# Second tile: the turning of batch 2's q waits for the remainder of its v, and the first tile's output is stored behind it

## The chip, the core and the metric

The kernel runs on one core of a Trainium2 chip. A core has a matrix engine (TensorE, PE in the profile, with PEld for its weight loads), a vector engine (DVE), a scalar engine (ACT), GpSimd (POOL) and a queue engine (SyncE, SP). Here POOL and SP mostly start transfers: POOL starts the loads, SP starts the stores and the transfers that transpose ("turn") 16-bit data on the way. The metric is the device time of one execution in microseconds.

## The reference

```python
# q, k, v: [8 batches, 8 heads, 576 rows, 64]; g_norm: [64]
kv  = einsum('bhsd,bhse->bhde', k, v)              # 64 x 64 for each batch and head
o   = einsum('bhsd,bhde->bhse', q, kv)
o   = o / sqrt(mean(o * o, axis=-1) + 1e-6) * g_norm
x   = o.transpose(0, 2, 1, 3).reshape(4608, 512)   # heads side by side
h   = x @ w_in                                     # 512 -> 2048
out = (h * sigmoid(1.702 * h)) @ w_out             # 2048 -> 512, float32
```

## The kernel before, in words

**Tiles.** A batch has 576 rows. Tiles t = 0 to 7 take 512 rows of batch t, tile 8 takes the 64 rows that are left of each of the eight batches. For every tile the kernel multiplies x by w_in (`Hidden` for tile 0, `SevenIn` from tile 1), applies the gate on ACT, and multiplies by w_out (`project_all` for tile 0, `Seven` from tile 1). From tile 1 on both products are done with seven half-size products in place of eight, which takes sums of quarters of the weights (`ws`, `tw`), of x (`xS`) and of the gated values (`gS`), made by DVE.

**Attention runs ahead.** While tile t is multiplied, pieces of the attention of batch t+1 and t+2 are put between the matmuls. The order is written out by hand: `manual_schedule`, and the dictionaries `u1` and `u2`. `at1(i, f)` calls f behind step i of the product with w_in, `at2(i, f)` behind matmul i of the product with w_out. Each engine runs its own instructions strictly in the order in which these calls emit them.

**What a batch from batch 2 on needs.** k and v are loaded by POOL into the two buffers `kraw` and `vbuf`, which all batches share. `load_kv` issues the main part (512 rows: line 115) and the remainder (64 rows: line 120); for batch 2 the main part comes in two halves. `kv_product` (line 247) multiplies k by v: 40 small matmuls, eight with the main rows and then two with the remainder for each pair of heads. q is loaded by `load_q` (line 143 for the main part, 149 for the remainder `qrem`) into `qraw` for even batches and `qbuf` for odd ones. SP turns the main part of q by `transpose_q` (line 290, into `qTd`) and the remainder by `transpose_rest` (line 294, into `qTr`). `rows` (line 332) multiplies the turned q by kv, `out` for the remainder is line 306. `turn` (line 362 on DVE, 368 on SP) scales the rows and turns them into `xT`, which is the next tile's x.

**The second tile, t = 1.** Steps 0 to 27 of its product with w_in are written in `SECOND`. Behind step 5 come `transpose_q` and `transpose_rest` of batch 2; at the step named `kv` stands the product of batch 2's k and v; behind step 22 POOL loads k, v and q of batch 3. In the product with w_out, `rows` of batch 2 stand behind matmul 19, its remainder behind 46, its `turn` behind 40 to 52; behind matmul 88 stands the k-v product of batch 3, behind 89 the loads of batch 4, behind 100 the turning of batch 3's q. In the third tile the k-v product of batch 4 stands behind matmul 15 of the product with w_out.

**Queues.** SP runs its transfers in this order around the change: the eight stores of tile 0 (`store_early(0)`, line 843, called at the end of `layers(0)`; 1 MB of float32 in all), the turning of batch 2's q and its remainder, the two `turn` transfers of batch 2's x, the turning of batch 3's q and remainder, the eight stores of tile 1. Loads from POOL are the software queue (q0) of the profile, transfers from SP and ACT the hardware queue (q1). Both run on the same 16 DMA engines. POOL has one marker form already, in later tiles: `after_turn` and `after_queries` (lines 127 and 131) copy one element of a turned buffer, so that the loads behind them are not issued until it has landed.

Of the kernel before, what the change touches and what calls it, by code (L numbers as in the profile page):

```python
# [16 lines left out]
def kernel(  # L17
# [10 lines left out]
    nc = tc.nc  # L28

    B, H, S, D = q.shape  # L30
# [11 lines left out]
    EARLY = 2  # L42
# [65 lines left out]
    kv_rows = {n: raw[n].rearrange("p c x -> p (c x)") for n in "kv"}  # L108
    RW = J * D
    RS = H * RW  # L110
# [26 lines left out]
    def q_rows(b):  # L137

        rows = qbuf if b % 2 else qraw.rearrange("p c x -> p (c x)")
        return rows[:, 0 : H * J * D]  # L140
# [14 lines left out]
    for n in "kqv":  # L155
# [11 lines left out]
        out=ident,  # L167
        in_=ident,
# [52 lines left out]
    class Attention:  # L221
# [63 lines left out]
                    r = slice(hl * D, (hl + 1) * D)  # L285
                    copy(self.engine, self.kb[to, c0:c1, half, 1 - hl], self.kvp[r, c0:c1, :])

        def transpose_q(self):
            self.qTd = attn.tile([P, H * J // 2, P], F16, name="qTd", tag="qTd", bufs=1)
            nc.sync.dma_start_transpose(out=self.qTd, in_=q_rows(self.b))  # L290

        def transpose_rest(self):
# [447 lines left out]
    def hid_seven(t, hid, seven, units1):  # L740


        xs = made.pop(t, None) or Sums(t, hid.x)
        todo = plan(t)
        parts = [SevenIn(hid, xs, g, todo) for g in range(len(PARTS))]

        def product(step):
            return parts[int(step[0])].product(int(step[1]))

        gates = []  # L750
        for n, step in enumerate(todo.steps):
            behind, gates = gates, []
            if step != "kv":
                gate = product(step)
                if gate:
                    gates.append(gate)
            for u in behind:
                u()
            for u in units1.get(n, ()):
                u()  # L760
            for i in range(4):
                if todo.xsums[i] == n:
                    xs.form(i)
            for i0, i1, which in todo.ready.get(n, ()):
                seven.sums(i0, i1, which)
        for u in gates:
            u()

        def late(step):
            gate = product(step)  # L770
            if gate:
                gate()

        left = {n: [lambda x=x: late(x) for x in steps] for n, steps in todo.late.items()}
        end = lambda: seven.sums(HF - 2, HF, 0)
        if left:
            left[max(left)].append(end)
        else:
            end()
        return left  # L780

    def layers(t, units1, units2):
        hid = d0 if t == 0 else Hidden(t)
        seven = Seven(t, hid.gT) if t else None
        left = hid_seven(t, hid, seven, units1) if t else first_columns(hid, units1)
        osbs[t] = opool.tile([P, 4, DM], F32, name="osb", tag="osb")
        if t:
            todo = {n: [lambda x=x: seven.sums(*x) for x in xs] for n, xs in plan(t).later.items()}
            for n, us in units2.items():
                todo.setdefault(n, []).extend(us)  # L790
            for n, us in left.items():
                todo[n] = us + todo.get(n, [])
            seven.run(todo)
        else:
            project_all(hid.gT, units2)
        if t < EARLY:
            store_early(t)
        elif t < B and t not in HALVED:
            store(t, 0, J)

    def first_columns(hid, units):

        for i, fo in enumerate(COLS):
            if i >= GROUP:
                for ko in range(KO):
                    hid.mm(ko, fo)
                hid.gate(fo)
            for u in units.get(i, ()):
                u()
# [166 lines left out]
    HALVED = (2, 3, 4, 5)  # L976
# [5 lines left out]
    for t in range(NT):  # L982
        b = t + 1
        u1, u2 = {}, {}

        def at1(i, f, *args):
            u1.setdefault(i, []).append(lambda: f(*args))

        def at2(i, f, *args):
            u2.setdefault(i, []).append(lambda: f(*args))  # L990

        def of(b, name, *args):
            return lambda: getattr(live[b], name)(*args)

        if t == 0:
            for l in range(2):
                at1(6, nc.vector.memset, kvd[l], 0.0)
            at1(7, of(0, "out", NPAIR))
            at1(7, scale_w_in, 0, 4)
            at1(7, w_in_sums, 0, 2)  # L1000
            at1(8, start, 1)
            at1(12, scale_w_in, 4, 6)
            at1(12, w_in_sums, 2, 3)
            at1(13, load_q, 2)
            at2(4, setattr, a0, "ss_pool", Attention.ss_pool)
            at2(4, of(0, "ss", NPAIR, True))
            at2(4, of(0, "apply", NPAIR))
            at2(18, weight_sum, 0, 0, HF)
            at2(18, scale_w_in, 6, 8)
            at2(18, w_in_sums, 3, 4)  # L1010
            for c in range(NPAIR):
                at1(12, of(1, "pack_q", c))
                at2(9 + 3 * c, of(1, "q", c))
                at2((36, 36, 49, 49)[c], of(1, "kv", c))
                at2((41, 43, 54, 55)[c], of(1, "out", c))
                at2((45, 50, 58, 60)[c], of(1, "ss", c))
                at2((48, 52, 58, 62)[c], of(1, "apply", c))
            for n in range(1, 4):
                at2(19, weight_sum, n, 0, 4)
                at2(38, weight_sum, n, 4, 6)  # L1020
            at2(39, load_kv, 2, 0, H // 2, False)
            at2(51, clear_rest)
            at2(51, load_kv, 2, H // 2, H)

            def first_sum():
                made[1] = Sums(1, xT[1])
                made[1].form(0)

            at2(55, first_sum)
        elif b < B:  # L1030
            todo = plan(t)
            at = todo.attn
            if t == 1:
                at1(todo.steps.index("kv"), of(b, "kv_all", "D"))
                at1(5, start, b)
                at1(5, of(b, "transpose_q"))
                at1(5, of(b, "transpose_rest"))
                at1(4, nc.scalar.preload_act_table_set, "gelu_apprx_sigmoid_and_others")
                for n, i in ((1, 8), (2, 11), (3, 16)):
                    at1(i, weight_sum, n, 6, HF)  # L1040
                at1(22, load_kv, 3)
                at1(22, load_q, 3)
                at2(88, start, 3)
                at2(88, of(3, "kv_all", "A"))
                at2(89, load_kv, 4)
                at2(89, load_q, 4)
            elif t + 2 < B:
                at2(at["rows"][0], start, t + 2)
                at2(at["rows"][0], of(t + 2, "kv_products"))
                at2(52, of(t + 2, "kv_copies", "A"))  # L1050
                if t + 3 < B:
                    at2(at["rows"][0], load_kv, t + 3, 0, H, False, "k")
                    at2(101, after_turn, b)
                    at2(101, load_kv, t + 3, 0, H, True, "v")
                    at2(101, after_queries, t + 2)
                    at2(101, load_q, t + 3)
            if t + 2 < B:
                at2(49 if t > 1 else 100, of(t + 2, "transpose_q"))
                at2(100, of(t + 2, "transpose_rest"))
            at2(at["table"], nc.scalar.preload_act_table_set, "abs_reciprocal_sqrt_and_small")  # L1060
            for h in range(2):
                at2(at["roots"][h], of(b, "roots", h))
            for j in range(J):
                if j < J // 2:
                    at2(at["rows"][j], of(b, "rows", j))
                for name in ("add_up", "turn"):
                    at2(at[name][j], of(b, name, j))
            rest = (80, 90, 96, 97) if 1 < t < B - 2 else (46, 74, 80, 82)
            at2(rest[0], of(b, "out", NPAIR))
            at2(rest[1], of(b, "ss", NPAIR))  # L1070
            at2(rest[2], of(b, "apply", NPAIR))
            at2(rest[3], nc.scalar.preload_act_table_set, "gelu_apprx_sigmoid_and_others")
        elif t < B:
            for name in ("ss_pool", "rest_pool"):
                at2(16, setattr, live[1], name, (ps_a, "att"))
            at2(16, of(1, "out", NPAIR))
            at2(34, nc.scalar.preload_act_table_set, "abs_reciprocal_sqrt_and_small")
            at2(44, of(1, "ss", NPAIR))
            at2(50, of(1, "apply", NPAIR))
            at2(52, nc.scalar.preload_act_table_set, "gelu_apprx_sigmoid_and_others")  # L1080
        layers(t, u1, u2)


# [28 lines left out]
```

## Time and profile before

| | |
|---|---|
| time, median of 3 runs | 259.11 us (258.80 to 259.48) |
| the profiled execution's own time | 259.74 us |
| span of that execution, first to last instruction | 258.0 us |
| outside the span in that execution | 1.74 us |
| busy share of the span: DVE, ACT, POOL | 75%, 69%, 22% |
| mean granted TensorE clock | 0.993 of full speed |
| DMA | 35.33 MB, mean 137 GB/s |

The views used below: the page (busy time by engine, and the chain of waits that ended last), the chain of waits in order of time (start in us from the beginning of the span, length in us, what), the timeline of one engine in a window (start, length, engine, line, operation), the list of DMA issues in a window (line, queue, count, KB of one, median us from issue to landing), and the stretches (in each of them the busy time of every engine, with the number of instructions, then the granted clock, the mean busy share of the DMA engines and GB/s; that share can exceed 1 because packets overlap on an engine). A length of an SP or POOL row of a transfer is the time that its issue took, not that of the transfer.

### The profile page before, as it was taken

The numbers are of one execution on the slowest core, as the hardware profiler recorded it, in microseconds if no ns is written. First come the engines' busy times: TensorE is split into PE (matmuls) and PEld (weight loads), VectorE is DVE, ScalarE is ACT, GpSimd is POOL, SyncE is SP. The second block draws the span as 40 slices with busy tenths as digits, with TensorE's granted clock in tenths as the row PEclk, the third lists the DMA queues.
The fourth block names the chain that finished last, engine by engine and source line by source line (L and its number), as shares of the span: only waits on it lengthen the run. The fifth ranks groups of instructions, "written<-read, shape, count | busy, mean of one in ns | idle before, by whom it ended". The sixth has DMA issues, their size and how long they took to land.

```text
span 258.0 us, 6355 instructions
## 1 busy us (share of the span) xinstructions
PE 251.7 (98%) x2596; PEld 204.4 (79%) x2596; DVE 193.9 (75%) x344; ACT 177.1 (69%) x322; POOL 57.0 (22%) x92
## 2 busy tenths in 40 slices
PE   8899999999999999999999999999999999999994
PEld 2444454788888888888888888898888888888883
DVE  1546685899958986798679867987799787857872
ACT  3458743988758894899579957995799469536800
POOL 8773244208061013301150134000000000000013
PEclk9979999999999999999999999999999999999999
DMA  7999999999989979996999699909500430012005
GB/s 181 194 188 206 204 204 197 216 216 115 184 159 208 221 91 224 153 158 81 186 184 164 84 205 135 190 5 136 202 4 0 84 163 3 0 57 108 3 19 145
DMA packets 68687, 35.33 MB, mean 137 GB/s; under 512 B 37970, under 2 KB 66258, under 8 KB 68402
## 3 DMA queue, kind: packets, MB, share of 16 engines
q0 software_dynamic: 37632, 18.31, 55.3%
q1 hardware_dynamic: 30624, 16.29, 27.4%
q8 instruction: 20, 0.33, 0.5%
q10 hardware_dynamic: 402, 0.33, 0.5%
q14 instruction: 9, 0.07, 0.1%
HBM read 36.70 MB, written 9.44 MB: 179 GB/s over the span
## 4 chain that ended last, share of the span: by engine, by line
PE 93%; DMA 4%; issue 0%; POOL 0%; DVE 0%
PE o L704 38%; PE h L584 38%; PE hT L473 6%; PE o L819 5%; DMA vbuf<-in_v_dram 2%; DMA qraw<-in_q_dram 2%; PE kvp L247 2%; PE outR L332 1%; PE ss L379 1%; PE outT L302 1%; PE q L454 0%; PE kvp L259 0%; PE outT L306 0%; PE kv L259 0%; DVE osb L684 0%
## 5 line engine op out<-in xcount | busy, mean ns | idle before, releaser
L561 ACT ACTIVATE gT<-h 128x512 f16<-128x512 f32 x96 | 52.5, 601 | 5.6 <-PE h L584 5.6
L584 PEld LDWEIGHTS <-ws 128*128 128x128 f16 x512 | 50.1, 98 | 5.9
L704 PEld LDWEIGHTS <-gS 128*128 128x128 f16 x512 | 49.1, 98 | 6.1 <-DVE gS L636 0.3
L584 PE MATMUL h<-xS,ws 128*128 128x256 f16 x384 | 52.2, 273 | 0.0
L704 PE MATMUL o<-tw,gS 128*128 128x256 f16 x384 | 45.6, 273 | 0.0
L584 PEld LDWEIGHTS <-w_in_sb 128*128 128x128 f16 x384 | 37.4, 98 | 4.7
L704 PEld LDWEIGHTS <-gT 128*128 128x128 f16 x384 | 37.6, 98 | 4.3
L704 PE MATMUL o<-w_out_sb,gT 128*128 128x256 f16 x256 | 31.4, 273 | 0.0
L584 PE MATMUL h<-xT,w_in_sb 128*128 128x256 f16 x224 | 31.1, 272 | 0.0
L681 DVE TENSOR_TENSOR osb<-o,qf 128x512 f32<-128x512 f32 (+1 forms) x25 | 16.7, 669 | 11.7 <-PE o L704 11.7
L598 DVE TENSOR_TENSOR h<-h,s 128x512 f32<-128x512 f32 x32 | 22.2, 698 | 4.2 <-PE h L584 2.6
L600 DVE TENSOR_TENSOR s<-h,s 128x512 f32<-128x512 f32 x32 | 22.1, 691 | 4.1 <-PE h L584 3.3
L738 POOL DMA_DIRECT2D out_dram<-osb x6 | 3.2, 537 | 93.2 <-DVE osb L681 93.2
L636 DVE TENSOR_TENSOR gS<-gT 128x512 f16<-128x512 f16 (+2 forms) x32 | 21.3, 685 | 0.6 <-ACT gT L561 0.6
L561 ACT ACTIVATE gT<-s 128x512 f16<-128x512 f32 x32 | 19.8, 628 | 2.4 <-DVE s L600 2.3
L530 DVE COPY s<-h 128x512 f32<-128x512 f32 x19 | 13.0, 686 | 8.2 <-PE h L584 8.2
L584 PE MATMUL h<-xS,w_in_sb 128*128 128x256 f16 x128 | 18.9, 273 | 0.0
L115 POOL DMA_DIRECT2D kraw<-in_k_dram x7 | 6.0, 853 | 56.9 <-PE kvp L247 52.0
L348 DVE TENSOR_REDUCE sum<-sq 128x8 f32<-128x512 f16 x24 | 14.9, 678 | 4.7 <-ACT sq L342 4.7
L320 ACT ACTIVATE sq<-outT 128x512 f16<-128x512 f32 (+1 forms) x16 | 7.9, 495 | 15.1 <-PE outT L302 9.5
L990 ACT ACT_TABLE_LOAD x14 | 18.0, 1283 | 0.2
L381 ACT ACTIVATE rs<-ss,eps_t 128x512 f32<-128x512 f32 (+1 forms) x16 | 9.2, 582 | 12.4 <-PE ss L379 12.3
(104 smaller groups left out, 373.9 us busy)
## 6 DMA issues: line engine op xcount, KB each, us to landing
out_dram<-osb SPq DMA_DIRECT2D x8, 512.0 KB, 4.6
kraw<-in_k_dram POOLq DMA_DIRECT2D x5, 512.0 KB, 6.0
vbuf<-in_v_dram POOLq DMA_DIRECT2D x5, 512.0 KB, 10.4
out_dram<-osb SPq DMA_DIRECT2D x2, 1024.0 KB, 4.9
qraw<-in_q_dram POOLq DMA_DIRECT2D x3, 512.0 KB, 11.6
qbuf<-in_q_dram POOLq DMA_DIRECT2D x3, 512.0 KB, 10.4
out_dram<-osb SPq DMA_DIRECT2D x6, 192.0 KB, 5.9
w_in_sb<-in_moe_w_in_dram POOLq DMA_DIRECT2D x2, 512.0 KB, 10.1
```

What stands on the lines that cost most here:

```text
L348: nc.vector.tensor_reduce(out=self.sum4[:, j, :], in_=self.o[j][1].rearrange("p (x d) -> p x d", d=D), op=ALU.add, axis=mybir.AxisListType.X,)
L473: nc.tensor.matmul(self.h[fo], w_in_sb[:, ko, fo * P : (fo + 1) * P], self.x[:, ko], start=(ko == 0), stop=(ko == KO - 1),)
L530: (nc.vector.tensor_copy if engine == "D" else nc.scalar.copy)(to, src)
L561: nc.scalar.activation(self.gT[:, to, n * TH : (n + 1) * TH], src, AFT.Gelu_apprx_sigmoid)
L584: nc.tensor.matmul(bank[name][:, a], w, x, start=(p in (1, 5) and a == 0 and k == 0), stop=(k == KH - 1), skip_group_check=True,)
L598: nc.vector.tensor_add(bank["z"], bank["x"], self.s5)
L600: nc.vector.tensor_add(self.s5, bank["x"], self.s5)
L636: op(s[:, n, lo], a, b)
L681: nc.vector.tensor_add(o, ps, self.kept[with_][:, m])
L704: nc.tensor.matmul(o, a, w, start=(p in (1, 2, 5) and i == 0 and (mo == 0 or split)), stop=(i == HF - 1), skip_group_check=True,)
L819: nc.tensor.matmul(os[mo], gT[:, fo, mo * P : (mo + 1) * P], w_out_sb[:, fo, :], start=(fo == 0), stop=(fo == FO - 1),)
L990: u2.setdefault(i, []).append(lambda: f(*args))
```

## The change

The eight stores of tile 0 are no longer issued at the end of tile 0. They are issued behind the turning of batch 2's q and remainder, in the second tile's step 5. And that turning waits: POOL copies one element of the remainder of batch 2's v (the last element of its first row in `vbuf`) into the first element of `qTd`. The copy needs the remainder of v to have landed, and the turning, which overwrites `qTd`, needs the copy done.

```diff
-        def transpose_q(self):
+        def transpose_q(self, after=None):
             self.qTd = attn.tile([P, H * J // 2, P], F16, name="qTd", tag="qTd", bufs=1)
+            if after is not None:
+                nc.gpsimd.tensor_copy(out=self.qTd[0:1, 0, 0:1], in_=after)
             nc.sync.dma_start_transpose(out=self.qTd, in_=q_rows(self.b))
...
-        if t < EARLY:
+        if t == 1:
             store_early(t)
-        elif t < B and t not in HALVED:
+        elif 1 < t < B and t not in HALVED:
             store(t, 0, J)
...
                 at1(5, start, b)
-                at1(5, of(b, "transpose_q"))
+                at1(5, of(b, "transpose_q", kv_rows["v"][0:1, RS + H * D - 1 : RS + H * D]))
                 at1(5, of(b, "transpose_rest"))
+                at1(5, store_early, 0)
```

In the instruction order of each engine this adds one copy on POOL, between the last load of batch 2 (line 120) and the first load of batch 3 (line 115). On SP the two turnings now stand ahead of the eight stores. The order on PE, DVE and ACT is the same. Two waits are new: the turning waits for the copy on POOL, and the load of the remainder of batch 3's v waits for the copy too, as the copy reads the buffer that it overwrites. `store_early(1)`, for tile 1, stays where it was.

## The prediction

> **What bounds the kernel now.** I read the busy shares first, then the chain of waits, then SP and POOL around the change, and last the DMA engines by stretches.
>
> ```profile
> span 258.0 us, 6355 instructions
> ...
> PE 251.7 (98%) x2596; PEld 204.4 (79%) x2596; DVE 193.9 (75%) x344; ACT 177.1 (69%) x322; POOL 57.0 (22%) x92
> ...
> PE 93%; DMA 4%; issue 0%; POOL 0%; DVE 0%
> ```
>
> PE is busy for 98% of the span, and the chain is PE for 93%; its 4% of DMA are the first loads. The chain in order of time, with the places where batches' k-v products (kvp), the turned q (outR, outT) and the turned x are first used:
>
> ```profile
> 47.96 9.21 PE h L584 x84
> 57.17 0.75 PE kvp L247 x40
> ...
> 63.33 0.57 PE outR L332 x32
> ...
> 67.12 0.12 PE outT L306 x4
> ...
> 71.93 0.75 PE kvp L247 x40
> ...
> 75.30 11.80 PE h L584 x108
> ...
> 89.28 0.75 PE kvp L247 x40
> ...
> 101.42 11.80 PE h L584 x108
> ```
>
> The second tile takes 75.30 - 47.96 = 27.34 us, the third 101.42 - 75.30 = 26.12. The second has one k-v product more (0.75), so 26.87 would be its length at the third's pace: 0.47 us is all that better transfers could win here. The change can hardly make the kernel faster; it can only keep PE fed or not. So I look for what comes late.
>
> SP's timeline, then POOL's:
>
> ```profile
> 46.27 4.38 SPq L843 DMA_DIRECT2D out_dram<-osb  x8
> 51.40 4.26 SPq L290 DMA_TRANSPOSE qTd<-qraw  x1
> 55.78 1.18 SPq L294 DMA_TRANSPOSE qTr<-qrem  x1
> 68.74 3.26 SPq L368 DMA_TRANSPOSE xT<-x  x2
> 72.17 1.92 SPq L290 DMA_TRANSPOSE qTd<-qbuf  x1
> 74.27 1.73 SPq L294 DMA_TRANSPOSE qTr<-qrem  x1
> ```
>
> ```profile
> 46.35 0.69 POOL L120 DMA_DIRECT2D vbuf<-in_v_dram  x1 [0.41 <-DMA qrem<-in_q_dram]
> ...
> 58.20 0.88 POOL L115 DMA_DIRECT2D kraw<-in_k_dram  x1 [11.16 <-PE kvp L247]
> ...
> 60.76 0.69 POOL L120 DMA_DIRECT2D vbuf<-in_v_dram  x1
> 61.43 0.90 POOL L143 DMA_DIRECT2D qbuf<-in_q_dram  x1
> ...
> 75.38 0.72 POOL L120 DMA_DIRECT2D vbuf<-in_v_dram  x1
> ...
> 104.33 0.18 POOL L131 COPY mark<-qTd 1x1 f16<-1x1 f16 x1 [1.55 <-DMA qTd<-qraw]
> ```
>
> How long single transfers took from issue to landing, from the DMA issues of narrow windows: the remainder of batch 2's v, issued at 46.35; q turned at 51.40, its remainder at 55.78; the remainder of batch 3's v (60.76) and q (61.43); x turned at 68.74 and, by the window asked, near 70.0; last the remainder of batch 4's v (75.38):
>
> ```profile
> vbuf<-in_v_dram POOLq DMA_DIRECT2D x1, 64.0 KB, 9.5
> ...
> qTd<-qraw SPq DMA_TRANSPOSE x1, 6.4
> ...
> qTr<-qrem SPq DMA_TRANSPOSE x1, 2.3
> ...
> vbuf<-in_v_dram POOLq DMA_DIRECT2D x1, 64.0 KB, 7.2
> ...
> qbuf<-in_q_dram POOLq DMA_DIRECT2D x1, 512.0 KB, 9.2
> ...
> xT<-x SPq DMA_TRANSPOSE x1, 4.5
> ...
> xT<-x SPq DMA_TRANSPOSE x1, 4.0
> ...
> vbuf<-in_v_dram POOLq DMA_DIRECT2D x1, 64.0 KB, 13.9
> ```
>
> Adding issue and duration gives slacks. Batch 2's v is whole at 55.85 and used from 57.17: 1.3 us. Turned q is there at 57.8, used at 63.33: 5.5 us. Its remainder at 58.1, used at 67.12: 9 us. Batch 3's v is whole at 68.0, used at 71.93: 3.9 us. Turned x is there at 73.2 and 74.0, used from 75.30: 2.1 us for the first; the second, as a DVE sum, only some matmuls later. Batch 4's v is whole at 75.38 + 13.9 = 89.28, and its product starts at 89.28, its first remainder matmul eight small matmuls later (8 x 0.75/40 = 0.15 us): a slack of about 0.1 us. That is the row that decides: whatever makes this load later is paid by PE at once.
>
> **The change part by part.**
>
> *Stores taken out of 46 to 56 us.* The stretches:
>
> ```profile
> 58.00:60.00 2.00, 2.00 (x20) 1.00 0.09 13
> ...
> 62.00:66.00 4.00, 4.00 (x64) 1.00 1.43 191
> ...
> 71.00:72.00 1.00, 1.00 (x17) 1.00 0.28 10
> ...
> 82.00:86.00 4.00, 4.00 (x39) 1.00 1.23 291
> ```
>
> and the queues' shares, first for 50 to 56 us, then for 62 to 66, then for 82 to 86:
>
> ```profile
> q1 hardware_dynamic: 1506, 1.26, 89.9%
> q0 software_dynamic: 1117, 0.19, 39.8%
> ...
> q0 software_dynamic: 1508, 0.76, 142.1%
> ...
> q1 hardware_dynamic: 512, 0.84, 65.6%
> q0 software_dynamic: 601, 0.31, 55.6%
> ```
>
> At 50 us the loads of batch 2 have 0.19 MB to go, which take until 55.85 beside the stores. Alone they move at 0.76/4 = 0.19 MB/us: 1 us, and about 1 us to the last landing, so v is whole near 52 (estimate; 51.3 to 55.85 as bounds, the later one being today's). PE gains nothing from that, as the product at 57.17 wasn't waiting.
>
> *The marker.* The POOL copy is 0.18 us (104.33). It waits on POOL from about 47, where POOL idles 11.16 us until 58.20 anyway; behind it stand batch 3's loads, which wait for PE. Cost 0; if v landed only after 58.2, each us would delay those loads by one. The wait of batch 3's v remainder for this copy is over long before.
>
> *The turnings.* They start about 0.4 us behind v, at 52.4 in place of 51.40, without stores in the way: issue 1.92 (72.17's row) to 4.26, landing 6.4 at most after the start, so q by 58.8 and its remainder about 0.3 behind, as now. Against 63.33 and 67.12 they have over 4 us. Cost 0; with v whole only at 55.85 the q would land at 62.7, still in time.
>
> *The eight stores, moved.* They are issued from 52.4 + 1.92 + 1.73 = about 56 (54.3 + 1.73), over 4.4 us, as at 46.27. SP is free by 60.5, the next turning of x waits for DVE until 68.74: 8 us of cover. What the stores meet on the DMA engines is the cost. Today those idle at 58 to 60 (share 0.09); the stores fill that hole. With data from about 58, as the turnings end, at the pace of issue (1.05 MB in 4.38 us, 0.24 MB/us), 0.5 MB is through by 60. The other 0.55 MB runs beside the loads of batch 3 that POOL issues from 58.20. In 82 to 86, when stores and loads also meet, stores move 0.84/4 = 0.21 MB/us and loads 0.31/4 = 0.078 instead of 0.19: each us costs the loads 0.112 MB, or 0.59 us. 0.55/0.21 = 2.6 us of that put the loads 1.5 us back. Bounds: 0.6 us, if only 0.2 MB is left at 60, to 3.0, if all 1.05 MB is.
>
> On this sharing the Trainium skill has a rule ("DMA: Bandwidth & Descriptors", Queues, rings and completion order): each DMA engine goes round robin between its queues, a packet from each. The trace half agrees: 512 to 601 packets in 82 to 86. At strictly one for one, a 2 KB store packet to a 512-byte load packet, an estimate by that rule gives the loads a fifth of 1.15/4 = 0.29 MB/us, 0.058; the stores' 0.55 MB would take 2.4 us and put the loads back 1.7 us, not 1.5.
>
> *Who is late next.* Batch 3's v would be whole at 69.5 (slack 3.9, nothing). Its q lands at 70.6 + 1.5 = 72.1, just when its turning is due (72.17). The x turnings meet 1.5 us more of loads; 2.1 us of slack holds. Then the queue goes on without rest: turned x, turned q, batch 4's loads from 76, the stores of tile 1. The one hole is 71 to 72 (share 0.28). If it is a true idle hole, it takes up 0.7 us; if it is a transfer waiting for the end of the loads, it moves with them and takes up nothing. I take 0.5, so batch 4's v is 1.0 us late, at 90.3, against a slack of 0.1: **PE waits 0.9 us at the k-v product of batch 4.** Bounds: 0.6 - 0.7 - 0.1 is no wait; 3.0 - 0.1 = 2.9 us. Later tiles run as before, as the next loads (batch 5) wait for that same product.
>
> *Sum.* 0 + 0 + 0 + 0.9 on the profiled execution's 259.74 (span 258.0 and 1.74 around it) is 260.64. That execution was 0.63 above the runs' median, so on the median 259.11 + 0.9 = **260.0 us**. The other end is a gain of at most 0.47: 258.6.
>
> **The rivals.**
>
> 1. *Not slower: the idle holes absorb it.* The 2 us at 58 to 60 and the 0.7 at 71 to 72 make room for 0.38 + 0.13 MB at 0.19, more at the stores' own pace; the loads are put back only 0.6 to 0.9 us and batch 4's v by 0 to 0.3. For it: the same bytes are moved, stores leave the crowded stretch before 56. Against: 0.1 us of slack. It decides if the stores are through by 61. Wait 0 to 0.3, time 259.1 to 259.4: 259.2.
> 2. *The turned x becomes the wait.* If the loads are put back over 2.1 us, the turning of x, issued at 68.74 into a full software queue, lands after 75.30, and PE waits there first. At 3.0 us: 0.9 us there, and 2.9 in all with batch 4's. For it: q's turning took 6.4 us at 51.40, beside other transfers, against 4.5 and 4.0 for x. Time 261.5 to 262.0.
> 3. *Faster.* Batch 2's v 3.8 us earlier could spare a wait in runs that had one at 57.17. This trace has none there; its whole reserve is 0.47 us. Time 258.6.
> 4. *The change doesn't do what it says:* v is whole at 55.9 even so, as its small packets are slow by themselves. Then the turnings start at 56.2, the stores at 60 with nothing of the hole used, and the loads go back the full 3 us: 262.0. Against: the same small transfer for batch 3 landed in 7.2 us, with a full 0.5 MB queue ahead.
>
> **How the numbers follow.** The forecast holds 0.45, rival 1 0.35, rival 2 0.09, rival 3 0.07, rival 4 0.04. 0.3% (0.78 us) is about what a measurement of this kernel can tell from no change, so slower means above 259.89, faster below 258.33. The forecast's wait lies between 0.5 and 1.6 us, 259.6 to 260.7, about 0.9 of it beyond the bound; with rivals 2 and 4 slower gets 0.53. Of rival 3 only 0.06 goes past the bound, as 0.47 doesn't reach it without a run-to-run gain besides. Same keeps 0.41. The range, 258.8 to 261.3, takes in rival 1 and half of rival 2, and leaves out the far ends of 2, 3 and 4.
>
> **What would show it.** In the profile of the changed kernel: the remainder of batch 2's v lands near 52 (step one); the turning of q starts on SP near 52.4 and takes about 2 us; the stores are issued from 56 to 60.5; the 58 to 60 stretch is no longer idle; batch 3's q lands near 72; the k-v product of batch 4 starts 14.9 us after its tile's first matmul, not 13.98 (89.28 - 75.30), with a wait for the load of v before it. I would be wrong if that distance stays 13.98 (rival 1), if the third tile itself begins more than 27.34 us after the second (rival 2), or if PE waits at 63.33 or 71.93, where I see cover of over 2 us.

## The result, and the profile after

| | before | after |
|---|---|---|
| median of 6 runs | 259.30 us (258.75 to 260.17) | 262.36 us (261.79 to 264.05) |
| the profiled execution's own time | 259.74 us | 263.33 us |
| its span | 258.0 us | 261.6 us |

The ratio is 1.0126, with a 95% interval of 1.0101 to 1.0151: about 3.1 us slower. The forecast was 260.0 in a range of 258.8 to 261.3, so the direction was right and the size too small.

First the page of the changed kernel, cut to busy shares and chain:

```profile
span 261.6 us, 6358 instructions
...
PE 252.2 (96%) x2596; PEld 204.5 (78%) x2596; DVE 194.2 (74%) x344; ACT 177.1 (68%) x322; POOL 57.3 (22%) x93
...
PE 88%; DMA 9%; POOL 1%; issue 1%; DVE 0%; DVEq 0%
```

PE has the same work (252.2 against 251.7 us busy), but it covers 96% of the span instead of 98%, and the chain has 9% of DMA where it had 4%. The chain in order of time shows the place:

```profile
47.17 9.21 PE h L586 x84
...
66.44 2.86 PE o L706 x27
69.30 9.98 DMA xT<-x
...
79.37 0.43 DVE xS L514
...
79.85 10.86 PE h L586 x92
...
92.89 0.75 PE kvp L247 x40
```

The step from 69.30 to 79.28 is a transfer: the second turning of batch 2's x, on which DVE's sum for the third tile waits. In the chain of the kernel before, no transfer stands in this stretch. The k-v product of batch 4 now starts 92.89 - 47.17 = 45.72 us after the second tile, before 89.28 - 47.96 = 41.32: 4.4 us more. The second tile itself began 0.79 us earlier in this execution, so the spans differ by 3.6 us. (In the profiled execution of before, the granted clock was 0.57 from 13 to 17 us, at the head; in this one it was 1.00 there, and 0.50 from 78 to 81 us, behind the wait.)

SP's timeline, then POOL's:

```profile
53.06 1.79 SPq L292 DMA_TRANSPOSE qTd<-qraw  x1
54.96 1.82 SPq L296 DMA_TRANSPOSE qTr<-qrem  x1
56.83 6.72 SPq L845 DMA_DIRECT2D out_dram<-osb  x8
67.94 6.08 SPq L370 DMA_TRANSPOSE xT<-x  x2
```

```profile
52.86 0.18 POOL L291 COPY qTd<-vbuf 1x1 f16<-1x1 f16 x1 [5.84 <-DMA vbuf<-in_v_dram]
57.40 0.89 POOL L115 DMA_DIRECT2D kraw<-in_k_dram  x1 [4.37 <-PE kvp L247]
```

The marker does what it says, and costs POOL nothing: it is through at 53.04, and batch 3's loads start at 57.40 behind PE as before. The turnings start at 53.06, the stores at 56.83. But the eight stores take 6.72 us to issue instead of 4.38, and the two turnings of x 6.08 instead of 3.26.

The DMA issues of narrow windows give the time to landing, in this order: the remainder of batch 2's v (issued at 46.33), batch 3's q (60.77), the last of the eight stores (63.04), the two turnings of x (67.94 and 69.30), the remainder of batch 4's v (74.59):

```profile
vbuf<-in_v_dram POOLq DMA_DIRECT2D x1, 64.0 KB, 6.5
...
qbuf<-in_q_dram POOLq DMA_DIRECT2D x1, 512.0 KB, 14.5
...
out_dram<-osb SPq DMA_DIRECT2D x1, 64.0 KB, 6.6
...
xT<-x SPq DMA_TRANSPOSE x1, 8.9
...
xT<-x SPq DMA_TRANSPOSE x1, 10.0
...
vbuf<-in_v_dram POOLq DMA_DIRECT2D x1, 64.0 KB, 12.6
```

Batch 2's v is whole at 52.8, batch 3's q only at 75.3 (before 70.6), and x at 76.8 and 79.3 (before 73.2 and 74.0). Batch 4's v is there at 87.2, long before PE comes to it at 92.89.

The stretches (PE busy time and instructions, granted clock, DMA share, GB/s), then the queues' shares for 60 to 64 and for 64 to 69 us:

```profile
58.00:60.00 2.00, 2.00 (x21) 1.00 0.67 135
60.00:64.00 4.00, 4.00 (x63) 1.00 1.17 149
64.00:69.00 5.00, 5.00 (x51) 1.00 1.27 248
...
72.00:76.00 4.00, 2.50 (x23) 1.00 1.51 120
...
78.00:81.00 3.00, 2.75 (x14) 0.50 1.41 191
```

```profile
q0 software_dynamic: 1151, 0.58, 116.4%
q1 hardware_dynamic: 8, 0.01, 1.0%
...
q0 software_dynamic: 1166, 0.45, 78.8%
q1 hardware_dynamic: 476, 0.78, 48.3%
```

Two things are to be seen. The stores did not share the engines with the loads from 60 us on: for 4 us they moved 0.01 MB, and some 0.78 MB (all that the hardware queue moved) went only from 64 to 69. And in 72 to 76 the engines are busier than in the same stretch of the kernel before, where only turnings ran, and move half as much (1.51 and 120 GB/s against 1.11 and 228):

```profile
72.00:76.00 4.00, 4.00 (x71) 1.00 1.11 228
```

PE is idle for 4.00 - 2.50 = 1.5 us of that stretch.

### The profile page after: what moved, and what is told of

Its sections match the earlier page's. It is cut to its first block, busy times and chain, and to the rows that moved or that the text cites. A ratio compares the mean times of both kernels' runs of the same rounds, so it can differ in the third digit from the quotient of the medians.

```text
span 261.6 us, 6358 instructions
## 1 busy us (share of the span) xinstructions
PE 252.2 (96%) x2596; PEld 204.5 (78%) x2596; DVE 194.2 (74%) x344; ACT 177.1 (68%) x322; POOL 57.3 (22%) x93
## 4 chain that ended last, share of the span: by engine, by line
PE 88%; DMA 9%; POOL 1%; issue 1%; DVE 0%; DVEq 0%
PE h L586 37%; PE o L706 36%; PE o L821 5%; PE hT L475 4%; DMA xT<-x 4%; DMA w_in_sb<-in_moe_w_in_dram 3%; DMA qraw<-in_q_dram 2%; PE kvp L247 1%; PE outR L334 1%; PE ss L381 1%; POOL w_in_sb L180 1%; PE kvp L259 0%; PE q L456 0%; PE outT L304 0%; PE outT L308 0%
## 5 line engine op out<-in xcount | busy, mean ns | idle before, releaser
L563 ACT ACTIVATE gT<-h 128x512 f16<-128x512 f32 x96 | 52.4, 601 | 5.7 <-PE h L586 5.6
L586 PE MATMUL h<-xS,ws 128*128 128x256 f16 x384 | 52.9, 275 | 0.3 <-DVE xS L514 0.3
L586 PE MATMUL h<-xT,w_in_sb 128*128 128x256 f16 x224 | 31.9, 277 | 2.4 <-DMA xT<-x 2.4
L532 ACT COPY h<-h 128x512 f32<-128x512 f32 x27 | 15.4, 576 | 4.6 <-PE h L586 4.4
```

What stands on the lines that cost most here:

```text
L532: (nc.vector.tensor_copy if engine == "D" else nc.scalar.copy)(to, src)
L563: nc.scalar.activation(self.gT[:, to, n * TH : (n + 1) * TH], src, AFT.Gelu_apprx_sigmoid)
L586: nc.tensor.matmul(bank[name][:, a], w, x, start=(p in (1, 5) and a == 0 and k == 0), stop=(k == KH - 1), skip_group_check=True,)
```

## The experiments

What was to be told apart, in the letters that the expectations use. A: the place of the stores is the cost. B: the wait of the turning is. C: the order on SP, stores behind turnings. D: the turning of batch 2's x crawls because the loads' queue still has work when it starts, however the work got there. E: the stores ahead of x in the hardware queue hold it up. F: the clock falls while PE waits, and that is a part of the loss. Ratios are to the kernel before on the same chip. A wait of PE is counted here from the time at which its next matmul was due at the pace of the others; the idle times that the profile prints are 0.1 to 0.2 us shorter.

**1. The marker alone.** Stores at the end of tile 0 again.

```diff
-        if t == 1:
+        if t < EARLY:
             store_early(t)
...
-                at1(5, store_early, 0)
```

> Only the marker: the stores of tile 0 are issued at the end of tile 0 again, the turning of batch 2's q still waits for the remainder of its v. Theory A (the place of the stores: 1 MB of them meets the loads of batch 3, which then end near 76 us instead of 71, and the turning of x behind them lands near 76.8 instead of 73.2): 259.3 +/- 0.6, turned x there by 74.5, no wait of PE. Theory B (the wait put on the turning is what costs): within 1 us of the changed kernel's 262.4.

Median 260.15 us, ratio 1.0040 (1.0009 to 1.0071). x came in time, as A says, but the time is 0.25 us above A's range: the marker and the later turning alone cost about a third of what the change costs (by the two intervals, the share is uncertain). The chain of this kernel has one transfer, the remainder of batch 4's v:

```profile
74.21 15.37 DMA vbuf<-in_v_dram
...
89.62 0.70 PE kvp L247 x32
```

32 of 40 small matmuls of that product come after it: the first eight ran, then PE waited for the remainder, 1.4 us. This is the wait that the forecast put into the changed kernel. In this execution batch 2's v, beside the stores, was whole only at 55.6, the turnings behind it ran into batch 3's loads, and the turning of batch 3's q, issued at 72.25, into batch 4's; which of these made the load late was not tried.

**2. The order alone.** No marker; the turnings start when q is there, the stores behind them.

```diff
-                at1(5, of(b, "transpose_q", kv_rows["v"][0:1, RS + H * D - 1 : RS + H * D]))
+                at1(5, of(b, "transpose_q"))
```

> Only the order: turning of batch 2's q and remainder ahead of the stores, without the wait for v. The turning can be issued from 46.4, the stores from about 52, five us earlier than in the changed kernel and before the loads of batch 3. Theory A: most of the loss is gone, 259.3 to 260.3. Theory C (what costs is that SP runs the stores behind the turnings, whenever that is): 262 or more.

259.01 us, ratio 0.9996 (0.9972 to 1.0020). The order costs nothing that can be measured: C falls. The new order alone costs nothing and the marker alone a third (1), so the whole loss takes both; the marker is what moves the stores from 52 to 57 us.

**3. No stores of tile 0.** Marker and turnings as in the changed kernel.

```diff
-                at1(5, store_early, 0)
```

> The changed kernel without the eight stores of tile 0; the first 512 rows of batch 0's output are not written, so 1 MB of transfers is left out. Theory A: no wait for the turned x, 259.0 +/- 0.6. Theory B: still 262 or more. If it is well below 259, the stores cost something in the kernel before as well.

258.94 us, ratio 0.9985 (0.9956 to 1.0014). The marker with the later turning is free when there are no stores, neither ahead of it nor behind: B falls. (In experiment 1, with the stores ahead, v was whole 2.9 us later than here, and the marker was not free.) And 1 MB less gains nothing that can be measured against before, so with this marker no placing of these stores could be expected to win more than the interval allows, 0.4%.

**4. Half of the stores early.**

```diff
+        if t == 0:
+            store_early(t, 0, 4)
...
-                at1(5, store_early, 0)
+                at1(5, store_early, 0, 4, 8)
```

> The changed kernel with the first four of the eight stores back at the end of tile 0, half of the bytes moved. Theory A with a loss that grows with the bytes: the wait for the turned x shrinks by about half, 260.3 to 261.3. If a slack is eaten first (about 2 us of the 3.6 us that x came late): little wait is left, 259.3 to 260. Theory B: 262.

262.24 us, ratio 1.0112 (1.0077 to 1.0148): nearly the whole loss with half of the stores moved, in the same place:

```profile
69.06 10.08 DMA xT<-x
```

Both guesses of A about the size were wrong: the cost isn't proportional to the bytes moved. It is no clean halving either. The four stores that stayed early held v back (the marker ran at 54.49), so the turnings came at 54.70 and the other four stores at 58.51 to 62.44, all 0.52 MB of them beside the loads; in the changed kernel about a quarter of the 1.05 MB had gone by 60. This led to D.

**5. The changed kernel without the main load of batch 3's q**.

```diff
-                at1(22, load_q, 3)
+                at1(22, load_q, 3, False)
```

> The changed kernel without the main load of batch 3's q (0.5 MB; tile 3's rows come from stale q). Stores and marker stay where the change put them. Theory D (the turning of batch 2's x crawls because the loads' queue still has work when it starts; how the stores got there doesn't matter): the loads end near 72 us instead of 76.6, turned x lands by 74, no wait at the third tile, 259.0 to 260.0. Theory E (the stores that stand ahead of x in the hardware queue hold it up): x still near 76.8, 262.

In place of the load, POOL sets the last 32 partitions of the buffer to zero, 1.80 us, and loads the remainder as before.

259.74 us, ratio 1.0024 (1.0003 to 1.0044). Most of the loss is gone. The eight stores are where the change put them, ahead of x, and x takes 4.8 and 4.3 us to land, nearly as before the change. (The profiled execution, 258.59 us, is the fastest of the ten and has no wait of PE; where the slower ones lose their time isn't shown.)

```profile
xT<-x SPq DMA_TRANSPOSE x1, 4.8
...
xT<-x SPq DMA_TRANSPOSE x1, 4.3
```

**6. The kernel before, with one load more:** 0.5 MB behind batch 3's q, into a buffer that nobody reads.

```diff
                 at1(22, load_q, 3)
+                at1(22, load_spare)
```

> The kernel before, stores in their old place, with one more load of 0.5 MB behind batch 3's q into a buffer that nobody reads. Theory D: the loads end near 74 us instead of 71, the turned x lands at 76 to 77 instead of 73.2 and 74.0, PE waits for it: 261 to 263 without any store moved. Theory E: no wait for x; at most the product of batch 4's k and v is late by the 2.7 us that 0.5 MB take, so up to 261.7, with the wait there.

261.44 us, ratio 1.0101 (1.0063 to 1.0138). No store was moved, and x is late all the same. Its landing times, and the chain, in which the second turning of x stands:

```profile
xT<-x SPq DMA_TRANSPOSE x1, 7.0
...
xT<-x SPq DMA_TRANSPOSE x1, 9.1
```

```profile
69.19 9.10 DMA xT<-x
```

5 and 6 settle it between D and E: it is the loads' queue, not the stores ahead of x. (D's landing times, 76 to 77, were not exact: x landed at 74.9 and 78.3.) The queues' packets in the same stretch, 70 to 74 us, of five kernels show how (packets, MB, share of the engines): before, changed, half of the stores early (4), without the q load (5), with one load more (6):

```profile
q1 hardware_dynamic: 2573, 0.64, 120.0%
q0 software_dynamic: 259, 0.03, 12.5%
...
q0 software_dynamic: 1235, 0.48, 109.9%
q1 hardware_dynamic: 379, 0.10, 41.7%
...
q0 software_dynamic: 1079, 0.32, 75.8%
q1 hardware_dynamic: 781, 0.20, 70.8%
...
q1 hardware_dynamic: 2922, 0.73, 104.6%
q0 software_dynamic: 10, 0.00, 0.4%
...
q0 software_dynamic: 753, 0.38, 69.7%
q1 hardware_dynamic: 747, 0.19, 66.9%
```

Where the loads are nearly through by 70 (0.03 or 0.00 MB left), the turnings move 0.64 to 0.73 MB in these 4 us. Where the loads still have 0.32 to 0.48 MB, turnings move 0.10 to 0.20 MB. In case 4 both queues together move 0.52 MB, less than the turnings alone. A packet of a turning costs more time there: 70.8% of 4 us on 16 engines for 781 packets is 58 ns, against 104.6% and 23 ns for 2922. In 6, 0.5 MB more, 2.7 us of loads at 0.19 MB/us, made the second turning of x take 9.1 us to land instead of 4.0.

Windows of 2 us take these 4 us apart. In each cell stands what the loads moved, then what the turnings moved, in MB:

| us | before | changed | half of the stores (4) | one load more (6) |
|---|---|---|---|---|
| 70 to 72 | 0.03, 0.13 | 0.39, 0.00 | 0.30, 0.07 | 0.37, 0.03 |
| 72 to 74 | 0.00, 0.51 | 0.08, 0.10 | 0.02, 0.13 | 0.01, 0.16 |
| 74 to 76 | 0.00, 0.40 | 0.04, 0.25 | 0.01, 0.18 | 0.17, 0.33 |

So there are two effects. While the loads run at full pace, the turnings of x hardly move: in the three slow kernels they were issued from 67.73 to 67.94 on, and move next to nothing until 71 or 72; in the kernel before, the loads are through at about 70 and the turnings start there. Then the first 2 us are slow in all four kernels (0.10 to 0.16 MB), and in the three slow ones the next 2 us as well (0.18 to 0.33 against 0.51), although the loads move little until batch 4's begin. The first effect is what D says. The second isn't a plain sharing with running loads, and no run shows what it is.

**7. The stores behind x.**

```diff
-                at1(5, store_early, 0)
+                at2(53, store_early, 0)
```

> The changed kernel with the eight stores behind the turning of batch 2's x instead of ahead of it. Theory D: x lands by 74, no wait at the third tile, but 1 MB more runs beside the loads of batch 4, whose product has 0.1 us of slack in the kernel before: the wait moves there, 3 to 5 us, 262 to 264. If moving them out of x's way is enough: 259.3.

260.45 us, ratio 1.0062 (1.0027 to 1.0098). x is in time, and the wait moves on, as D says; the time is below its range. In the profiled execution batch 4's product waits 0.7 us and the products with batch 3's turned q another 1.0, the transfer in the chain:

```profile
77.37 13.96 DMA qTd<-qbuf
```

**8. Batch 4's product later.** The kernel before, with that product and the load of k behind it after matmul 32 instead of 15.

```diff
-                at2(at["rows"][0], of(t + 2, "kv_products"))
+                kv_at = 32 if t == 2 else at["rows"][0]
+                at2(kv_at, of(t + 2, "kv_products"))
```

> The kernel before with the k-v product of batch 4 behind matmul 32 instead of 15 of the third tile's product with w_out, 1.9 us later, so that its loads have a slack of about 2 us instead of 0.1. If the tightest point of the kernel before is that product, the slower of its executions (260 to 261) lose their wait: median 258.5 to 259.0, ratio 0.998 +/- 0.002. If it isn't: 259.1, no change.

259.41 us, ratio 1.0011 (0.9992 to 1.0029): no gain. The slack of 0.1 us isn't what sets the kernel's median. The profiled execution had another wait, 0.6 us for the remainder of batch 2's v, the one that the change's early v takes away:

```profile
45.95 10.67 DMA vbuf<-in_v_dram
...
56.67 0.69 PE kvp L247 x32
```

**9. The changed kernel once more,** with the next three.

> The changed kernel once more, beside the next three on the same chip. Theory D: 262.4 +/- 0.6, turned x there near 76.8, some 4 us behind the kernel before. Theory F (2.5 us of PE idle sometimes makes the granted clock fall to a half, and the matmuls after the wait take 213 ns instead of 110 for 3.4 us): where the profile shows such a stretch behind the wait, its execution is 1.2 to 1.7 us above one with the same wait and none.

262.41 us, ratio 1.0127 (1.0095 to 1.0160). This profiled execution (262.43 us, granted clock 1.000 all through) has the same two waits, 1.9 us for the first turning of x and 1.6 for the second, in sum 3.5, the second with this step in the chain:

```profile
69.09 9.72 DMA xT<-x
```

The times tell something on F as well. Three of the four executions had a granted clock of 1.000 and took 262.17 to 262.43 us; the seven of the kernel before on this chip had 0.997 to 1.000 and a median of 259.30. So the whole loss of about 3 us is there without any low clock. The fourth, at 0.993, took 263.72: a low clock comes on top where it occurs.

**10. Loads of batch 3 behind the stores.** Four small POOL writes, which need the stores landed, ahead of the loads.

```diff
+                at1(22, lambda: [nc.gpsimd.memset(osbs[0][0:P, mo, 0:1], 0.0) for mo in range(4)])
                 at1(22, load_kv, 3)
```

> The changed kernel with four small POOL writes ahead of batch 3's loads that need the stores of tile 0 landed. Without loads beside them the eight stores should land by 62.5 instead of 69.7, 5 us after their first issue. The loads start near 62 instead of 58 and end near 74 to 75: theory D has x still crawl behind them, landing at 75.5 to 77, 261 to 263. If the stores' 6 us standstill behind the loads were the whole loss: x by 74.5 and below 260.

267.03 us, ratio 1.0295 (1.0263 to 1.0328), above every expectation. The stores did land early: the last took 2.3 us instead of 6.6. But the loads, issued only from 64.2, then ran into the turnings of x, and PE waited 4.0 us for batch 3's k and v and 2.7 more for the remainder of v:

```profile
out_dram<-osb SPq DMA_DIRECT2D x1, 64.0 KB, 2.3
```

```profile
66.72 10.77 DMA vbuf<-in_v_dram
```

Of these 6.7 us, the later issue (64.17 instead of 57.40, less the slack of 3.9 us that the forecast read for this v) makes about 2.9; the remainder of v also took 10.8 us to land instead of 7.2. So the meeting is bad for both: loads that run beside a turning are late too. From 74 to 78 us the two queues moved 1168 and 1162 packets.

**11. Idle matmuls into the wait,** 22 in the third tile's first bank, ahead of the first matmul that needs x.

```diff
                 self.open(name)
+                if self.fill and p == 1 and self.g == 2:
+                    for _ in range(22):
+                        nc.tensor.matmul(bank[name][:, 0], kvb[1][:, 0, :], ..., start=True, stop=True)
```

> The changed kernel with 22 idle matmuls (2.4 us at full clock) into the first product's bank of the third tile, ahead of the first matmul that needs the turned x, so that PE is busy while it waits. Theory F: no half clock behind the wait; median 261.3 to 262.0, the executions above 263 gone. If the clock plays no part: 262.4 as before, or up to 2.4 more where x isn't late.

263.23 us, ratio 1.0147 (1.0109 to 1.0184). No gain, three of its four executions are above 263, and with what experiment 9 shows F is not a regular part of the loss (the idle matmuls, 2.4 us, are some tenths longer than the first wait and may cost these themselves). In the profiled execution no half clock follows the wait, and the chain still hangs on the second turning of x.

**12. Batch 3's q behind the turned x.**

```diff
-                at1(22, load_q, 3)
...
+                at2(70, after_turn, 2)
+                at2(70, load_q, 3)
                 at2(89, load_kv, 4)
```

> The changed kernel with batch 3's q loaded only after the turned x of batch 2 has landed (a POOL marker, as the later tiles have it). Theory D: x lands by 74 as without that load, no wait at the third tile; but the loads of batch 4 stand behind 0.5 MB more, and their product waits 1 to 3 us: 260 to 262. Theory E: x still near 76.8.

262.34 us in two runs (261.29 and 263.39), ratio 1.0114 (1.0058 to 1.0171), 0.3 us above D's range. x lands at 72.5 and 73.3, as D says and E doesn't. PE then waits elsewhere: 0.4 us for the remainder of batch 3's v, 1.1 for that of batch 4's, 1.2 for the turned q of batch 3, which is now loaded late. The first and the last are in the chain:

```profile
60.06 11.53 DMA vbuf<-in_v_dram
...
79.55 12.33 DMA qTd<-qbuf
```

## Why the prediction was wrong

*What bounds.* Right: PE was fed without gaps, the change could not gain, and it lost where a transfer came late.

*Marker, turnings of q, SP's order.* Right for the changed kernel. v was whole at 52.8 (forecast 52), the turning started at 53.06 (52.4) and was issued in 1.79 us, the stores started at 56.83 (56). The order is free by itself (2), and so is the marker where v isn't held up by the stores (3); where it is, the marker costs 0.4% (1).

*What the stores cost the loads.* Mis-sized. The forecast had 0.5 MB of stores through by 60 and the rest sharing with the loads, which would put the loads back 1.5 us, 3.0 at most. Measured, batch 3's q was whole at 75.3 instead of 70.6: 4.7 us (from issue to landing 14.5 instead of 9.2). The stores stood still from 60 to 64 (0.01 MB) and went from 64 to 69. A standstill is what the forecast had no term for, and it wasn't free for the loads: they moved 0.58 MB in these 4 us, in experiment 3, without stores, 0.72. From 64 to 69 they moved 0.45 MB instead of 0.93. Together that is 0.62 MB, at 0.19 MB/us 3.3 us (an estimate from these rows). The rest of the 4.7 seems to fall where the loads then met the turnings. The sharing that was read from 82 to 86 us held roughly once the stores moved (0.16 MB/us of them and 0.09 of loads).

The rule of the Trainium skill that was weighed there ("DMA: Bandwidth & Descriptors", Queues, rings and completion order: a packet from each queue in turn) fits 64 to 69 us half (476 packets to 1166) and not 60 to 64 (8 to 1151); measured packets decide. It fits 80 to 84 us of the changed kernel, where the turning of batch 3's q runs beside the loads of batch 4: 975 packets to 969, 0.25 MB to 0.48. Whether a packet of the trace is what the rule means by one, no run shows.

*Who is late next.* This is the step that failed: "The x turnings meet 1.5 us more of loads; 2.1 us of slack holds." The loads went on for more than 1.5 us longer, and a turning doesn't merely come later by as much. Until the loads' main flow ended, at about 72 us instead of 70, the turnings of x moved nothing, and then they went on more slowly: 0.34 MB in the 4 us from 72, where in the kernel before turnings moved 0.64 in the 4 us from 70. x came 3.6 and 5.3 us late against a slack of 2.1. Half of the stores (4) and a single load more (6) made for most of the same loss, so it isn't proportional to the bytes; whether there is an edge, and where, no run shows. A row that pointed at it was there in before: the turning of q at 51.40, beside other transfers, needed 4.26 us to issue and 6.4 to land, and the forecast used it for rival 2 only.

*The wait.* Put at batch 4's k-v product, 0.9 us. In the changed kernel it was at the third tile's first matmuls: rival 2's place, at 1.9 + 1.6 = 3.5 us (experiment 9). Rival 2 had 0.9 there, and 2.9 with batch 4's product. Batch 4's product, with PE late, had slack again. Where x was kept in time, that product was often the next to wait: 1.4 us in experiment 1, 0.7 in 7, 1.1 in 12, none in the profiled executions of 2, 3 and 5.

*Rival 1*, idle holes that absorb the stores, fell: the hole at 58 to 60 took 135 GB/s, and about a quarter of the stores had gone by 60. *Rival 3* needed a wait for batch 2's v in the kernel before. There is one at times (0.6 us in the profiled execution of 8), too small to be seen in the change's result. *Rival 4* fell with v at 52.8.

What stays open is why the stores stood still from 60 to 64 us. With the loads held back (10) they didn't, so the loads have to do with it; how, no run shows. Open too is why the turnings of x stayed slower than in the kernel before once the loads' main flow had ended.

## What to carry to other kernels

A transfer that is moved out of a crowded stretch is paid where it lands. Look there not only for bytes and slack, but for a transposing transfer that will now overlap a running load queue; here 2.7 us of loads more made such a transfer 5.1 us slower. A marker that holds one transfer also holds everything behind it on the same queue: here a new order that is free alone (2) and a marker that costs 0.4% alone (1) cost 1.3% together. When half of a suspected cost gives nearly the whole loss, stop scaling it; see whether what was left behind does harm of its own, and look for the next transfer that all variants delay.

## What the runs showed that was not expected

- Turnings and loads together moved less than turnings alone: 0.52 MB from 70 to 74 us (experiment 4) against 0.73 (experiment 5). For the first 2 us these were mostly loads, and in the other 2 both queues together moved 0.15 MB.
- A queue with transfers issued can stand still: eight stores, issued from 56.83 to 63.55, moved 0.01 MB from 60 to 64 us beside the loads.
- In the changed kernel's first profiled execution the granted clock was 0.50 from 78 to 81 us, behind 2.4 us in which PE waited, and matmuls there took up to 417 ns instead of 272. In experiment 9's execution, with a wait of 1.9 us and one of 1.6, it stayed at 1.00, and its time was 0.90 us lower (262.43 against 263.33), less than the 1.2 to 1.7 that F expected.
